# Two query tiles that share their gate and up projections in the tail of a transformer block

## The chip, the cores and the metric

The kernel runs on one core of a Trainium2 chip. The metric is the device time of one execution in microseconds; the figure given for a kernel is the median of its runs. The engines are called TensorE (PE in the profile; its weight loads are PEld), VectorE (DVE), ScalarE (ACT), GpSimd (POOL) and SyncE (SP, which issues the DMAs).

## What is computed

One transformer block with modulated layer norms, over 2048 tokens of width 512, with 32 heads of 16 and a gated MLP of width 1792, all in bf16. Cut to what matters:

```python
mod = (silu(c) @ w_mod).reshape(1, 6, 1, 512)
sa, ca, ga, sb, cb, gb = [mod[:, i] for i in range(6)]
h = layernorm(x) * (1 + ca) + sa
q, k, v = split_heads(h @ wqkv)                  # 32 heads of 16
p = softmax(q @ k.T * 16 ** -0.5)
x = x + ga * ((p @ v) @ wo)
h = layernorm(x) * (1 + cb) + sb
x = x + gb * ((gelu(h @ w_gate) * (h @ w_up)) @ w_down)
```

## The kernel before

The 2048 tokens are 16 tiles of 128. Queries are taken in six sets of 512, 512, 512, 256, 128 and 128 tokens (`SETS`, tiles 0-3, 4-7, 8-11, 12-13, 14 and 15). The heads are taken eight at a time by position in their group of four (`qd` 0 to 7). The last two sets run together over 256 columns for `qd` 0 to 5 and apart for 6 and 7. A unit of work, a set and a `qd`, is cut into score banks: one PSUM bank of 128 keys or more by 512 columns. There are six score banks (`ps_sc`), used three by three: while TensorE fills three, ScalarE takes the exponential of the other three in one ACTIVATE to the SBUF ring `E` of 24 slots. Two more banks are `ps_pv`, which gathers P times V for a unit, and `ps_mi`, which everything else shares.

Some groups of four score banks (a "quad") don't go to ScalarE: VectorE converts the scores to 16-bit integers with a scale and an offset, which read as bf16 are an approximate exponential; three further copies with shifted offsets, on VectorE or GpSimd, average the error. Which groups go this way is decided as the program is made.

The program's order is not written out by hand. A recorder keeps every instruction with its reads and writes and a rough model of when each engine would be free (`model`, `cost`). The function `stream` picks, position by position (`pos` counts score banks), what TensorE does next: the next scores, P times V of a bank that is done, a piece of side work, or a filler matmul that is thrown away (`short` asks whether the last 3.4 us had enough of them). Side work (`plan`) are generators: projections of the first half, the output projection (`side_wo`), the second layer norm and the MLP of each query set (`side_ffn`), all in the bank `ps_mi`, one after the other. A credit grows with each position and is spent with each piece of side work. VectorE's and GpSimd's pieces are `tasks`, a list of steps each; `step` takes the ready one with the lowest `urgency`.

What follows the last scores is `tail`. It has two generators, and goes on with what is left of the side work. At each turn it takes the matmul that can start first; the first generator has 300 ns of preference. With `self.whole` set, matmuls use the full array in place of four column strips. The names that matter there: `ka` is tile 14, `kb` is tile 15. `TCOL` gives their columns in the transposed norm `t2T` (256 and 384, next to each other), `prods` are their gated products, `wg`, `wu` and `wd` the resident weights of gate, up and down, loaded long before. For tile 14 the LN statistics come in the main stream; its four transposes are the side entry `side_ffn(k, EARLY)` with `EARLY = 0`, in `ps_mi`, and VectorE scales and shifts the result into `t2T`. For tile 15 `tail_end` makes the last two reciprocals (`near_end`), the output projection on top of x in score bank 4, LN, and four transposes in score bank 5 and `ps_mi`. `tail_ffn` is run for each tile by itself: chunks of four 128-column blocks of the MLP (the last of two), for each a gate bank, an up bank, ScalarE's GELU, VectorE's product, and the down matmuls of the chunk before. `down_fin` scales the sum with `gb`, adds it to x and stores the tile.

Of the kernel before, what the change touches and what calls it, by code (L numbers as in the profile page):

```python
# [5 lines left out]
ACT = mybir.ActivationFunctionType  # L6
ALU = mybir.AluOpType
BF16 = mybir.dt.bfloat16
# [5 lines left out]
P = 128  # L14
# [7 lines left out]
NFC = F // P  # L22
# [25 lines left out]
PREFER = 300  # L48
# [20 lines left out]
FLOW = NA - 2  # L69
URGENT = 6  # L70
LAG = 40
EARLY = 0
BACK = 8
END = (0, None)

# [31 lines left out]
class _Recorder:  # L107
# [181 lines left out]
    def model(self, op, t, cost):  # L289
        eng = op.eng  # L290
        if op.stream not in COMPUTE:
            self.free[eng] = t + 460
            early = t < 20000
            self.dma_free = max(t + 1400, self.dma_free) + cost / (350 if early else RATE)
            op.t1 = self.dma_free + (1500 if early else LAND)
        elif eng == "pe":
            cols, rows, tp = cost
            mode = 0 if tp is None else (1 if rows == 32 else 2)
            t = max(t, self.pe_issue)
            if self.fetched[0] % 128 == 0 and t > 20000:  # L300
                t = self.fetched[1] = max(t, self.fetched[1] + 3750)
            self.fetched[0] += 1
            if mode != self.pe_mode:
                t = max(t, self.pe_end + 105)
            q = range(16)
            if mode == 1:
                q = range(tp[0] // 8, tp[0] // 8 + 4)
            elif mode == 2:
                q = range(tp[1] // 32, 16, 4)
            t = max(t, max(self.tile_free[i] for i in q))  # L310
            end = t + max(cols, 64) / 2.4
            for i in q:
# [159 lines left out]
class _Kernel(_Recorder):  # L472
# [485 lines left out]
            self.task(steps[:1], ("rs", gi), self.after([("st2", t) for t in tiles]))  # L958
            self.task(steps[1:], ("ln2", gi), self.after([("rs", gi)] + [("ffn", gi - 1)] * (0 < gi <= FLOW) + [("ffn", FLOW)] * (gi > FLOW + 1)))

    def side_ffn(self, gi, part=None):

        q0, W = SETS[gi]
        n = W // P
        tiles = [q0 // P + i for i in range(n)]
        mi = self.mi[:, :]
        c0, t0 = BCOL[gi], TCOL[gi]
# [3 lines left out]
        kpb = 512 // W  # L971
        chunks = []
# [16 lines left out]
            load(0, i)  # L989
            load(1, i)  # L990
        yield from self.until(("ln2", gi))
        if part is not None:
            for i in range(5):
                yield from self.until(("ld", "u", i))
        for h in range(2):
            yield from self.side_t(lambda t: self.normed(gi, t), n, h,
                                   lambda dc: self.t2T[:, dc, t0:t0 + W], self.modB)
# [29 lines left out]
        def U(ci):  # L1027
# [8 lines left out]
            for b0 in range(0, m, kpb):  # L1036
# [7 lines left out]
                    self.tt("dve", prod[:, fcs[0]:fcs[0] + m, c0:c0 + W], w.rearrange("p (k n) -> p k n", k=m),  # L1044
                            g.rearrange("p (k n) -> p k n", k=m), ALU.mult)
                yield END
        nch = len(chunks) if part is None else part
        for i in range(3):
            load_down(i)
        for ci in range(nch + 1):  # L1050
# [4 lines left out]
            if ci >= 1:  # L1055
                yield from U(ci - 1)
                if ci >= nch - 1:
                    load_down(5 + ci - nch + 1)
        if part is not None:
            self.done(("part", gi))  # L1060
            return
        wd = self.wdst if flow else self.wd
        for i in range(0 if flow else 7):
            yield from self.until(("ld", "d", i))
# [12 lines left out]

    def urgency(self, tk):

        if tk[1] is None or tk[1][0] in ("den", "ld"):  # L1080
            return -1
        if tk[1][0] != "shift":
            return 1
        return 0 if self.plain[tk[1][1]] <= (URGENT if tk[1][1][3] == 512 else URG2) else 2
# [58 lines left out]
    def plan(self, ends, nsplit):  # L1143
# [19 lines left out]
        w.append((lambda: self.near_end(k, 6, self.mi[:, 0:P]), s0, s0, True))  # L1163
        w.append((lambda: self.near_end(k, 7, self.mi[:, 0:P]), s0, s0, True))
        w.append((lambda: self.side_wo(k), s0, s0, True))
        w.append((lambda: self.side_ffn(k, EARLY), s0, n - 20, True))
        res = []
        for mk, s, e, *early in w:
            self.dry = True
# [58 lines left out]
    def stream(self):  # L1228
# [133 lines left out]
        while cg <= group[units[-1]]:  # L1362
# [95 lines left out]
            if hot:  # L1458
                pv_do(hot[0])
                continue  # L1460
            if ok[0] and (ok[1] or self.pe_mode == 2 or tq is None or not mem) and not (side and self.credit > 1536 and tq is not None):
                pv_do(tp[0])
                continue
            if side:
# [131 lines left out]
    def tail(self, ka, kb):  # L1596

        self.whole = True
        self.act(self.tcol[:, 0:1], self.tcol[:, 0:1], ACT.Gelu_apprx_tanh)
        gens = [self.tail_end(kb), self.tail_ffn(ka, self.pv[:, :], range(0, 4), 0)]  # L1600
        nxt = [None] * len(gens)
        while True:
            t = self.pe_now()
# [3 lines left out]
            for i, g in enumerate(gens):  # L1607
                if g is None:
                    continue
                if nxt[i] is None:  # L1610
                    nxt[i] = next(g, 0)
                if nxt[i] == 0:
                    gens[i] = None
                elif nxt[i] is not None:
                    x = max(self.probe(nxt[i]), t + 30) - (PREFER if i == 0 and ("x1", kb) not in self.have else 0)
                    if best is None or x < best[0]:
                        best = x, i
            w = self.next_side()
# [18 lines left out]
            f, nxt[best[1]] = nxt[best[1]], None  # L1637
            f()

    def tail_end(self, k):  # L1640
        q0, W = SETS[k]
        assert W == P
        c0, tile = BCOL[k], q0 // P
# [12 lines left out]
        while self.work:  # L1656
            yield None
        for h in range(2):
            pb = (self.scp[:, 5, :], self.mi[:, :])[h]
            yield lambda h=h, pb=pb: self.transp(pb, lambda t: self.normed(k, t), 1, h)  # L1660
            for i in range(2):
                dc = 2 * h + i
                self.modulate(("act", "dve")[h], self.t2T[:, dc, TCOL[k]:TCOL[k] + W],
                              pb.bitcast(BF16)[:, W * i:W * i + W], self.modB, dc)
        yield from self.until(("x1", k))
        yield from self.tail_ffn(k, self.mi[:, :], (5, 4, 0, 1, 2, 3), 4)

    def tail_ffn(self, k, down, banks, e0):
        q0, W = SETS[k]
        c0, tile, kpb = BCOL[k], q0 // P, 512 // W  # L1670
        chunks = [range(a, min(NFC, a + kpb)) for a in range(0, NFC, kpb)]
        nb = [0]

        def up(ci, w):
            if nb[0] == 2 and k == len(SETS) - 1:
                yield from self.until(("p", k - 1, len(chunks) - 1))
            bk = self.scp[:, banks[nb[0] % len(banks)], :]
            nb[0] += 1
            for s, fc in enumerate(chunks[ci]):
                for dci in range(NDC):  # L1680
                    yield lambda s=s, fc=fc, dci=dci: self.up_mm(bk[:, W * s:W * s + W], w, fc, TCOL[k], W, dci)
            return bk
        first = 0
        if k < len(SETS) - 1:
            first = EARLY
            yield from self.until(("part", k))
        for ci in range(first):
            for fc in chunks[ci]:
                yield lambda fc=fc: self.down_mm(down, c0 // P, fc)
        for ci in range(first, len(chunks) + 1):  # L1690
            if ci < len(chunks):
                n = len(chunks[ci])
                g = self.E[:, e0 + ci, 0:W * n]
                bg = yield from up(ci, self.wg)
                self.task([("act", lambda bg=bg, g=g, n=n: self.act(g, bg[:, 0:W * n], ACT.Gelu_apprx_tanh))],
                          ("g", k, ci))
                bu = yield from up(ci, self.wu)
                yield from self.until(("g", k, ci))
                self.task([lambda bu=bu, g=g, n=n, f0=chunks[ci][0]: self.stt(
                    self.prods[c0 // P][:, f0:f0 + n, :], bu[:, 0:W * n].rearrange("p (k n) -> p k n", k=n), 2.0,  # L1700
                    g.rearrange("p (k n) -> p k n", k=n), ALU.mult, ALU.mult)], ("p", k, ci))
            if ci > first:
                yield from self.until(("p", k, ci - 1))
                if k == len(SETS) - 1:
                    self.done("down")
                for fc in chunks[ci - 1]:
                    yield lambda fc=fc: self.down_mm(down, c0 // P, fc)
        self.task([lambda: self.down_fin(down, tile)], None)


def bass_adaLN_cond__mha_block__geglu_ffn__prompt_kernel(
# [41 lines left out]
```

The softmax here doesn't subtract the row's maximum and nothing guards it: scores larger than these inputs give would overflow.

## Time and profile before

| | us |
|---|---|
| median of 5 runs (lowest to highest) | 809.32 (807.74 to 809.80) |
| the profiled execution | 809.32 |
| its span | 807.3 |
| TensorE busy | 753.0 (93%) |
| ScalarE busy | 769.7 (95%) |
| VectorE busy | 688.8 (85%) |
| GpSimd busy | 262.3 (32%) |
| last exponential ends at | 775.7 |
| last PV matmuls end at | about 777.0 |
| last matmul, by the modelled end | 803.7 |
| last store issued at | 805.1 |

The span goes from the first to the last instruction that the profile holds; 2 us lie around it. The 40 slices show three stages: a start of some 20 us with the loads at 311 GB/s, a long stretch in which ScalarE is at 9 tenths in every slice, and the last slice and a half, in which ScalarE has little to do:

```profile
PE   8999999999899998999989999999999999998988
PEld 3333333322222222222222222222333333354556
DVE  6878998987898899989898899998898897879753
ACT  4999999999999999999999999999999999999951
```

A tail of 30 us in a span of 807 is hard to see there; the stretches and the chain of waits cut by time show it.

### The profile page before, as it was taken

The page shows a single profiled execution, that of the slowest core. Times are in us where ns is not written, and L with a number is a line of the kernel's source. Part 1 is how long each engine was busy: PE and PEld are TensorE (multiplying, and loading weights), DVE is VectorE, ACT ScalarE, POOL GpSimd, SP SyncE. Part 2 cuts the span into 40 slices and gives each one's busy share as a digit, 9 for nine tenths or more (in the row PEclk, how much of TensorE's full clock was granted, in tenths as well). Part 3 has the DMA queues.
Part 4 walks back from the last instruction along what each step waited for, and adds up shares of the span by engine and source line. Part 5 has one row for each costly group of instructions (what it writes and reads, how often), then busy time and mean ns, then how long its engine had stood idle before and what let it go on. Part 6 is the DMA issues. An engine that isn't in the chain of part 4 may idle for free.

```text
span 807.3 us, 27653 instructions
## 1 busy us (share of the span) xinstructions
PE 753.0 (93%) x12359; PEld 272.8 (34%) x12359; DVE 688.8 (85%) x1252; ACT 769.7 (95%) x733; POOL 262.3 (32%) x162
## 2 busy tenths in 40 slices
PE   8999999999899998999989999999999999998988
PEld 3333333322222222222222222222333333354556
DVE  6878998987898899989898899998898897879753
ACT  4999999999999999999999999999999999999951
POOL 2100427282655351424436551333425000002100
PEclk9999999999999999999999999999999999999999
DMA  9100000000022111210022021120122221120000
GB/s 311 57 9 11 16 10 16 11 17 10 15 61 62 35 55 35 61 42 19 26 58 71 25 59 41 49 55 23 39 68 75 65 73 37 43 68 14 20 10 15
DMA packets 58617, 36.05 MB, mean 45 GB/s; under 512 B 17961, under 2 KB 55074, under 8 KB 58498
## 3 DMA queue, kind: packets, MB, share of 16 engines
q1 hardware_dynamic: 56114, 32.71, 14.8%
q8 instruction: 97, 1.59, 0.8%
q10 hardware_dynamic: 2384, 1.57, 0.7%
q14 instruction: 22, 0.18, 0.1%
HBM read 29.62 MB, written 2.61 MB: 40 GB/s over the span
## 4 chain that ended last, share of the span: by engine, by line
ACT 83%; PE 12%; DVE 3%; DMA 1%; issue 0%; SPq 0%; DVEq 0%
ACT E L379 80%; PE ps_sc L366 6%; PE ps_mi L366 3%; ACT wreg L379 3%; PE ps_pv L366 2%; DMA mreg<-in_w_mod_dram 1%; DVE mreg L391 1%; DVE wreg L383 0%; DMA rb<-scr_rec 0%; DVE dreg L391 0%; SPq L430 0%; DVE wreg L391 0%; DVE xs L383 0%; DVE hreg L391 0%; PE ps_sc L370 0%
## 5 line engine op out<-in xcount | busy, mean ns | idle before, releaser
L379 ACT ACTIVATE E<-ps_sc 128x1024 bf16<-128x1024 f32 (+2 forms) x686 | 742.4, 1267 | 15.7 <-PE ps_sc L366 13.6
L391 POOL TENSOR_SCALAR mreg<-dreg 128x2048 uint16<-128x2048 uint16 x93 | 175.1, 1897 | 270.9 <-DVE mreg L391 114.0
L391 DVE TENSOR_SCALAR dreg<-ps_sc 128x512 uint16<-128x512 f32 x258 | 174.8, 686 | 31.3 <-PE ps_sc L366 29.5
L366 PE MATMUL ps_sc<-qT,kme 32*128 32x512 bf16 (+2 forms) x1311 | 172.0, 332 | 15.1 <-ACT E L379 13.5
L366 PE MATMUL ps_sc<-qT,kmo 32*128 32x512 bf16 (+2 forms) x1316 | 173.3, 331 | 10.5 <-ACT E L379 9.7
L366 PE MATMUL ps_pv<-E,vaug 128*17 128x512 bf16 (+2 forms) x2096 | 148.9, 327 | 1.2 <-DVE vaug L400 0.8
L366 PE MATMUL ps_pv<-mreg,vaug 128*17 128x512 bf16 (+2 forms) x1768 | 124.9, 338 | 1.2 <-DVE mreg L391 0.5
L391 DVE TENSOR_SCALAR mreg<-ps_sc 128x512 uint16<-128x512 f32 x134 | 91.0, 685 | 15.3 <-PE ps_sc L366 14.8
L391 POOL TENSOR_SCALAR mreg<-mreg 128x2048 uint16<-128x2048 uint16 x38 | 71.6, 1897 | 96.1 <-DVE mreg L391 55.7
L366 PE MATMUL ps_mi<-wreg,mreg 128*32 128x512 bf16 (+1 forms) x1280 | 91.8, 372 | 2.3 <-DVE wreg L396 0.7
L366 PEld LDWEIGHTS ps_sc<-qT,kme 32*128 32x128 bf16 x1311 | 45.4, 91 | 139.4 <-ACT E L379 111.2
L366 PEld LDWEIGHTS ps_sc<-qT,kmo 32*128 32x128 bf16 x1316 | 45.8, 91 | 130.9 <-ACT E L379 110.4
L391 DVE TENSOR_SCALAR mreg<-dreg 128x2048 uint16<-128x2048 uint16 x123 | 81.1, 685 | 0.5 <-PE ps_pv L366 0.4
L366 PEld LDWEIGHTS ps_pv<-E,vaug 128*17 128x17 bf16 x2096 | 44.2, 89 | 58.1 <-issue 46.5
L366 PEld LDWEIGHTS ps_pv<-mreg,vaug 128*17 128x17 bf16 x1768 | 40.3, 89 | 35.0 <-issue 10.9
L391 DVE TENSOR_SCALAR mreg<-mreg 128x2048 uint16<-128x2048 uint16 x73 | 47.9, 684 | 4.2 <-PE ps_pv L366 4.1
L643 POOL TENSOR_SCALAR mv<-mv 128x4 f32<-128x4 f32 (+2 forms) x10 | 2.7, 269 | 128.9 <-DVE mv L423 121.5
L366 PEld LDWEIGHTS ps_mi<-wreg,mreg 128*32 128x32 bf16 x1280 | 27.3, 95 | 40.1 <-issue 16.8
L366 PE MATMUL ps_mi<-hreg,wreg 128*32 128x512 bf16 x480 | 39.9, 384 | 0.4 <-DVE vaug L400 0.2
L366 PE MATMUL ps_sc<-xs,ident 128*32 128x512 bf16 x353 | 28.9, 401 | 11.4 <-ACT E L379 11.2
L400 DVE CAST wreg<-ps_mi 128x512 bf16<-128x512 f32 x49 | 33.6, 685 | 5.8 <-PE ps_mi L366 5.6
L396 DVE SCALAR_TENSOR_TENSOR wreg<-wreg,ps_mi 128x512 bf16<-128x512 bf16 x49 | 33.4, 681 | 4.6 <-PE ps_mi L366 3.0
(151 smaller groups left out, 692.8 us busy)
## 6 DMA issues: line engine op xcount, KB each, us to landing
mreg<-in_B_w_up_dram SPq DMA_DIRECT2D x22, 256.0 KB, 3.0
mreg<-in_B_w_gate_dram SPq DMA_DIRECT2D x15, 256.0 KB, 3.0
rb<-scr_rec SPq DMA_DIRECT2D x96, 32.0 KB, 1.8
dreg<-in_B_w_down_dram SPq DMA_DIRECT2D x9, 256.0 KB, 3.3
mreg<-in_w_mod_dram SPq DMA_DIRECT2D x1, 2048.0 KB, 14.5
mreg<-in_B_w_down_dram SPq DMA_DIRECT2D x8, 256.0 KB, 2.7
out_dram<-xs SPq DMA_DIRECT2D x16, 128.0 KB, 1.7
osb<-osb SPq DMA_DIRECT2D x48, 32.0 KB, 2.0
```

Source lines behind the costliest of these rows:

```text
L366: return self.rec("pe", lambda e: e.matmul(out, lhsT, rhs, start=start, stop=stop, tile_position=tp), [lhsT, rhs], [out], cost=(n, int(rhs ...
L379: return self.rec("act", lambda e: e.activation(out, in_, func, scale=scale, **kw), rd, wr, cost=self.cost("act", out, [in_], "act"))
L391: return self.rec(eng, lambda e: e.tensor_scalar(out, a, s1, s2, **kw), rd, [out], cost=self.cost(eng, out, [a], "ts"))
L396: return self.rec("dve", lambda e: e.scalar_tensor_tensor(out, a, s, b, op0=op0, op1=op1), rd, [out], cost=self.cost("dve", out, [a, b], " ...
L400: return self.rec(eng, lambda e: e.tensor_copy(out, in_), [in_], [out], cost=self.cost(eng, out, [in_], "ts"))
L643: self.rec("pool", lambda e: e.tensor_scalar(v, v, EPS, None, op0=ALU.add), [v], [v], cost=200)
```

## The change

Tile 14's transposes leave the side work and become `tail_t`, which tile 15 uses too: tile 14 in score banks 1 and 2, tile 15 in 5 and 3. Tile 14's scaling and shifting moves to ScalarE. There is one `tail_ffn` for both tiles. It runs at most `SOLO = 2` stages of four blocks for tile 14 alone, as long as tile 15's transposes are not there; then the same stages for tile 15 alone; then the rest in stages of two blocks, with tiles 14 and 15 side by side as 256 moving columns. Down matmuls stay apart by tile, tile 14's in `ps_pv`, tile 15's in `ps_mi`, and tile 15's wait until the side work is over.

Around it: `urgency` puts tile 15's reciprocals, normalised heads and LN steps first on VectorE in the tail; the tail's first generator keeps its preference to the end; in the last `CLOSE = 48` positions of the stream, ready P times V is no longer held back for side work; and the planner's model counts a matmul of 128 columns or more on the full array as at least 160 columns and a shorter one as at least 64 (before: at least 64 for both).

The model's line reads `max(cols, 64 if mode or cols < P else 160)`, where `mode` is 0 for the full array.

```diff
-EARLY = 0
+SOLO = 2
+CLOSE = 48
...
-            end = t + max(cols, 64) / 2.4
+            end = t + max(cols, 64 if mode or cols < P else 160) / 2.4
...
     def urgency(self, tk):
 
+        if self.whole and tk[1] is not None and tk[1][0] in ("rec", "onorm", "ln2") and tk[1][1] == len(SETS) - 1:
+            return -2
...
-        w.append((lambda: self.side_ffn(k, EARLY), s0, n - 20, True))
...
-            if ok[0] and (ok[1] or self.pe_mode == 2 or tq is None or not mem) and not (side and self.credit > 1536 and tq is not None):
+            if ok[0] and (ok[1] or self.pe_mode == 2 or tq is None or not mem) and not (side and self.credit > 1536 and tq is not None and pos < nseq - CLOSE):
...
-        gens = [self.tail_end(kb), self.tail_ffn(ka, self.pv[:, :], range(0, 4), 0)]
+        gens = [self.tail_end(kb), self.tail_ffn(ka, kb)]
...
-                    x = max(self.probe(nxt[i]), t + 30) - (PREFER if i == 0 and ("x1", kb) not in self.have else 0)
+                    x = max(self.probe(nxt[i]), t + 30) - (PREFER if i == 0 else 0)
...
+    def tail_t(self, k, banks):
+
+        yield from self.until(("ln2", k))
+        for h in range(2):
+            pb = self.scp[:, banks[h], :]
+            yield lambda h=h, pb=pb: self.transp(pb, lambda t: self.normed(k, t), 1, h)
+            for i in range(2):
+                dc = 2 * h + i
+                self.modulate(("act", "dve")[h * (k == len(SETS) - 1)], self.t2T[:, dc, TCOL[k]:TCOL[k] + P],
+                              pb.bitcast(BF16)[:, P * i:P * i + P], self.modB, dc)
+        self.done(("t2", k))
...
-        while self.work:
-            yield None
-        for h in range(2):
-            pb = (self.scp[:, 5, :], self.mi[:, :])[h]
...
-        yield from self.until(("x1", k))
-        yield from self.tail_ffn(k, self.mi[:, :], (5, 4, 0, 1, 2, 3), 4)
+        yield from self.tail_t(k, (5, 3))
+
+    def tail_ffn(self, ka, kb):
+
+        yield from self.tail_t(ka, (1, 2))
+        for i in range(5):
+            yield from self.until(("ld", "u", i))
+        nb = [0, 0]
+        count = {ka: 0, kb: 0}
+        downs = {ka: self.pv[:, :], kb: self.mi[:, :]}
+
+        def up(w, fcs, ks):
+            c, W = TCOL[ks[0]], P * len(ks)
+            banks = (0, 1, 2, 5, 3, 4) if ("x1", kb) in self.have else (0, 1, 2)
+            bk = self.scp[:, banks[nb[0] % len(banks)], :]
+            nb[0] += 1
+            for s, fc in enumerate(fcs):
+                for dci in range(NDC):
+                    yield lambda s=s, fc=fc, dci=dci: self.up_mm(bk[:, W * s:W * s + W], w, fc, c, W, dci)
+            return bk
+
+        def split(x, fcs, ks, i):
+            return x[:, 0:P * len(fcs) * len(ks)].rearrange("p (k t n) -> p k t n", t=len(ks), n=P)[:, :, i, :]
+
+        def down(fcs, ks, e):
+            yield from self.until(("p", e))
+            for k in ks:
+                while k == kb and self.work:
+                    yield None
+                if k == kb:
+                    self.done("down")
+                for fc in fcs:
+                    i = count[k]
+                    count[k] += 1
+                    yield lambda k=k, fc=fc, i=i: self.mm(downs[k], self.prods[BCOL[k] // P][:, fc, :],
+                                                          self.wd[fc // 2][:, fc % 2, :], start=i == 0, stop=i == NFC - 1)
+                if count[k] == NFC:
+                    self.task([lambda k=k: self.down_fin(downs[k], SETS[k][0] // P)], None)
+
+        def stage(fcs, ks, last):
+            e, n = nb[1], len(fcs) * len(ks) * P
+            nb[1] += 1
+            g = self.E[:, e, :]
+            bg = yield from up(self.wg, fcs, ks)
+            self.task([("act", lambda: self.act(g[:, 0:n], bg[:, 0:n], ACT.Gelu_apprx_tanh))], ("g", e))
+            bu = yield from up(self.wu, fcs, ks)
+            yield from self.until(("g", e))
+            self.task([lambda i=i, k=k: self.stt(self.prods[BCOL[k] // P][:, fcs[0]:fcs[-1] + 1, :], split(bu, fcs, ks, i), 2.0,
+                                                 split(g, fcs, ks, i), ALU.mult, ALU.mult) for i, k in enumerate(ks)], ("p", e))
+            if last:
+                yield from down(*last)
+            return fcs, ks, e
+        last, alone = None, []
+        for a in range(0, 4 * SOLO, 4):
+            if ("t2", kb) in self.have:
+                break
+            alone.append(range(a, a + 4))
+            last = yield from stage(alone[-1], (ka,), last)
+        yield from self.until(("t2", kb))
+        yield from self.until(("x1", kb))
+        for fcs in alone:
+            last = yield from stage(fcs, (kb,), last)
+        for a in range(4 * len(alone), NFC, 2):
+            last = yield from stage(range(a, a + 2), (ka, kb), last)
+        yield from down(*last)
```

More of the change, by code (lines that the diff above doesn't have):

```diff
@@ L959, in side_wo, with side_ffn @@
             self.task(steps[1:], ("ln2", gi), self.after([("rs", gi)] + [("ffn", gi - 1)] * (0 < gi <= FLOW) + [("ffn", FLOW)] * (gi > FLOW + 1)))
-    def side_ffn(self, gi, part=None):
+    def side_ffn(self, gi):
         q0, W = SETS[gi]
@@ L991, in side_ffn @@
         yield from self.until(("ln2", gi))
-        if part is not None:
-            for i in range(5):
-                yield from self.until(("ld", "u", i))
         for h in range(2):
@@ L1046, in U @@
                 yield END
-        nch = len(chunks) if part is None else part
+        nch = len(chunks)
         for i in range(3):
@@ L1058, in side_ffn @@
                     load_down(5 + ci - nch + 1)
-        if part is not None:
-            self.done(("part", gi))
-            return
         wd = self.wdst if flow else self.wd
@@ L1642, in tail_end @@
         assert W == P
-        c0, tile = BCOL[k], q0 // P
+        tile = q0 // P
         bank = self.scp[:, 4, :]
@@ L1655, in tail_end @@
         self.task([("act", lambda: self.act(self.xs[:, tile, :], bank, ACT.Copy))], ("x1", k))
-        while self.work:
-            yield None
-        for h in range(2):
-            pb = (self.scp[:, 5, :], self.mi[:, :])[h]
[L1660 to L1664, printed above, removed]
@@ L1665, in tail_end @@
-        yield from self.until(("x1", k))
-        yield from self.tail_ffn(k, self.mi[:, :], (5, 4, 0, 1, 2, 3), 4)
[L1668 to L1676, printed above, removed]
+        yield from self.tail_t(k, (5, 3))
@@ L1677, in up @@
+    def tail_ffn(self, ka, kb):
[8 more added lines that the diff above has]
+            banks = (0, 1, 2, 5, 3, 4) if ("x1", kb) in self.have else (0, 1, 2)
             bk = self.scp[:, banks[nb[0] % len(banks)], :]
             nb[0] += 1
-            for s, fc in enumerate(chunks[ci]):
+            for s, fc in enumerate(fcs):
@@ L1680, in up @@
                 for dci in range(NDC):
-                    yield lambda s=s, fc=fc, dci=dci: self.up_mm(bk[:, W * s:W * s + W], w, fc, TCOL[k], W, dci)
+                    yield lambda s=s, fc=fc, dci=dci: self.up_mm(bk[:, W * s:W * s + W], w, fc, c, W, dci)
             return bk
[L1683 to L1704, printed above, removed]
-                    self.done("down")
-                for fc in chunks[ci - 1]:
-                    yield lambda fc=fc: self.down_mm(down, c0 // P, fc)
@@ L1708, in tail_ffn @@
-        self.task([lambda: self.down_fin(down, tile)], None)
+        def split(x, fcs, ks, i):
[6 more added lines that the diff above has]
+                if k == kb:
+                    self.done("down")
+                for fc in fcs:
[5 more added lines that the diff above has]
+                    self.task([lambda k=k: self.down_fin(downs[k], SETS[k][0] // P)], None)
```

## The prediction

> **What bounds the kernel now.** I read the page's chain of waits first, then ScalarE's busy time over the long middle stretch, then the last 30 us in three views: busy time with granted clock by stretch, the chain in order of time, and TensorE's timeline.
>
> ```profile
> ACT 83%; PE 12%; DVE 3%; DMA 1%; issue 0%; SPq 0%; DVEq 0%
> ...
> 25.00:775.72 750.72, 706.65 (x11697) 244.41 (x11698) 657.42 (x1174) 748.35 (x700) 254.26 (x144) 1.00 0.14 38
> 777.00:780.20 3.20, 3.18 (x27) 1.51 (x15) 2.81 (x6) 0.23 (x2) 0.00 (x0) 1.00 0.03 5
> 780.20:783.20 3.00, 0.85 (x7) 0.43 (x7) 2.55 (x9) 0.00 (x0) 0.80 (x2) 1.00 0.13 44
> 783.20:786.60 3.40, 3.38 (x32) 3.16 (x32) 1.34 (x4) 1.89 (x4) 0.00 (x0) 0.51 0.00 0
> 786.60:803.70 17.10, 17.09 (x225) 13.53 (x222) 5.92 (x10) 3.75 (x7) 0.00 (x0) 1.00 0.01 2
> 752.50:764.30 11.80, 10.31 (x290) 5.28 (x293) 8.44 (x17) 11.67 (x12) 3.79 (x2) 1.00 0.07 15
> ```
>
> The columns of the stretches are start:end, length, then busy time of TensorE, its weight loads, VectorE, ScalarE and GpSimd, the granted clock, DMA share and GB/s. From 25 us to 775.72 us ScalarE is busy for 748.35 of 750.72 us: the exponentials set the time, and only 2.4 us of it are gaps. ScalarE's last exponential ends there. After it TensorE sets the end, and it has two losses. Between 780.2 and 783.2 us it works for 0.85 of 3.00 us: a **hole** of 2.15 us. In the next 3.4 us it is busy all the time, but at a granted clock of 0.51: 3.38 x 0.49 = 1.66 us lost. From 786.6 to 803.7 us it is full, at full clock.
>
> The chain in order of time (start, length, what) says who holds the hole open:
>
> ```profile
> 779.10 0.66 PE ps_mi L366 x3
> 779.77 0.02 issue
> 779.79 0.70 DVE wreg L383
> 780.49 0.02 issue
> 780.51 0.42 DVE xs L383
> 780.94 0.62 DVE st L419
> ...
> 781.76 0.49 DVE wreg L391 x2
> 782.26 0.05 issue
> 782.30 0.30 PE ps_mi L370 x2
> ...
> 791.36 1.79 PE ps_sc L366 x32
> 793.15 0.86 PE ps_pv L366 x4
> ```
>
> Tile 13's last down matmuls in the bank `mi` end, its two closing VectorE operations follow, and only then can tile 14 (`ka`) have its transposes in `mi`, each pair waiting for VectorE to scale and shift the one before. Yet tile 14's norm was written by 775.05 us (the 0.41 us operation on VectorE that starts at 774.64). So tile 14's projections, ready in principle, begin only at 782.43, beside tile 15's own LN chain, whose transposes start at 784.00. The last two lines give prices: 32 full-array matmuls of 128 columns take 1.79 us, **56 ns** each; four of 512 take 0.86, **215 ns** each.
>
> **The change, part by part.** The profiled execution took 809.32 us, span 807.3, and 809.32 is also the median shown, so I subtract from 809.32 directly.
>
> Removed: the side entry that made tile 14's transposes in `mi`. The four transposes, and four VectorE operations of 0.28 to 0.35 us, leave VectorE between 781.68 and 783.22; the same four transposes come back in the tail, into score banks 1 and 2, with four ScalarE operations. The last exponential has left those banks at 775.72 and the table load is over at 777.02, so the transposes can follow the last PV matmuls at 777.0 (0.3 us, the row at 782.30). ScalarE's row for this work, two in 0.80 us from 784.53, mean 456 ns, steps by 0.34: four take 3 x 0.34 + 0.46 = 1.5 us, so tile 14 is ready at about 777.5 + 1.5 = 779.0. ScalarE is idle from 777.24 to 784.04, so this costs nothing; without that cover it would be 1.5 us.
>
> Fill: tile 14 goes alone through up to two stages of four chunks, 64 matmuls x 56 ns = 3.58 us, and one stage's four down matmuls, 0.86: 4.44 us of work that exists from 779.0 on. The other work of TensorE up to the hole (two reciprocal sums, 0.68; identity and output projection, 0.86 + 0.43; tile 13's down matmuls, 1.08; the transposes, 0.3) is 3.35 us from 777.07. Together they reach 777.07 + 3.35 + 4.44 = 784.9, past tile 15's transposes at 784.0. So the hole can close: **-2.15**. With no stretch of low activity I also expect the clock to hold: **-1.66**. The row for that is 752.5 to 764.3, where TensorE is busy 10.31 of 11.80 us, with waits of 0.48 to 0.74 us, at clock 1.00.
>
> The Trainium skill, "TensorE: Matmul & The Clock Gate", section "Why this matters for your kernels", speaks against that second gain: it puts the fall to half rate down to idle gaps of over about 3 us, and the longest single gap here is 1.48 us. Taken by the letter the half clock has another cause, and the time would be 1.66 us above my sum. The trace has 1.23 busy us in the 3.4 before the fall, so I go by low activity in a window.
>
> Sharing: the last six chunks of both tiles run as three stages of 16 matmuls over 256 columns, 48 in place of 96. No full-array row of 256 columns is shown; bounds are 56 and 215 ns. The nearest row is the column-split form (`ps_mi<-wreg,mreg 128*32 128x256`, x32 from 748.58 to the next start at 749.46): eight full equivalents in 0.88 us, 110 ns. 48 x 0.110 = 5.28 against 96 x 0.056 = 5.38: **-0.1**, at most -2.7 and at worst +4.9 by the bounds; I take the nearest row, since two of 128 cost the same 112.
>
> The same page, section "Back-to-back issue gap", gives about 81 ns for a 128-column matmul in a stream with weight loads, and 262 cycles for 256 columns. As an estimate from it, sharing would save 2.5 us and not 0.1. The row says 56 ns with weight loads in between, so the page's price isn't met here.
>
> Given back: (a) Now both tiles end together. The last down matmuls of `ka` end 0.43 us before `kb`'s, and `ka`'s closing pair on VectorE (0.70 + 0.03 + 0.42, rows at 802.65 and 803.38) stands ahead of `kb`'s. Before, the last VectorE end was 805.05, 1.36 after TensorE's modelled end at 803.69; now -0.43 + 1.15 + 0.1 + 1.15 = 1.97 after it: **+0.6**. (b) The last stage's two products (0.42 us rows of 128x256, 0.36 apart, with 0.07 and 0.1 around them: 0.95) must be done before its downs, and the previous stage's four downs cover 0.86: **+0.1**. (c) Tile 15's scaled transposes come 1.3 us after its transposes start (784.00 to 785.33), that is between 784.4 and 785.3; the fill ends between 784.4 and 784.9. A stall of 0 to 0.9: **+0.4**, the middle. If fillers cover it the clock is safe, but not the time.
>
> The urgency edit lets tile 15's reciprocals, norms and LN steps go first on VectorE. Tile 13's closing pair (780.86 could be 780.25) and tile 14's scalings (0.3) stood in the chain; a product of 0.69 us can now stand there instead. Bounds -0.9 to +0.7; taken as 0, because TensorE has work for that time anyway. What queues behind the new wait of the joint stages (`t2` and `x1` of tile 15) is tile 15's and the shared work on TensorE alone.
>
> Letting PV go ahead of side work in the last 48 positions only reorders. Best: fewer than the 64 PV matmuls (0.89 us) remain after the last exponential, at most -0.5. Worst: the nine down matmuls of tile 13 that now run before 777 slip behind, 9 x 0.215 = +1.9. I take 0, nearest to a swap of equal work. A transpose priced at 160 columns in the planner is no instruction; it shifts planned times and can reshuffle the long stretch. There, gaps could yield at most 2.4 us, or a group of four score banks could move between ScalarE and VectorE. By the page's exp rows (412.7/420 for two banks, 372.3/257 for three: 0.48 a bank) a group is worth **1.9 us**. Sign unknown; I take 0.
>
> DMAs, GpSimd operations and SP's queue keep their number: nothing is moved past them but the two output stores, both now at the end and already overlapping (1.59 us for both).
>
> Sum: -2.15 - 1.66 - 0.1 + 0.6 + 0.1 + 0.4 = **-2.8**: 806.5 us, span 804.5.
>
> **Rivals.**
> (1) *The exponentials grow*. The reshuffled plan hands fewer score banks to VectorE, which is 85% busy with no rule that keeps the number. Each lost group costs 1.9 us of an engine that has 2.4 us of gaps in 750. One gives 808.4; from two (810.3) the change is slower than before; three give 812.2. Against it: a 14 ns shift per transpose is small beside any 1.1 us exponential.
> (2) *The hole stays in part*: tile 14's gates come late, or tile 15's chain gets products in front of it. With 1.1 us of hole and the half clock left: -1.05 - 0.1 + 0.7 = -0.4, so 808.9. For it: TensorE's order is fixed in advance by modelled times. Against: 4.4 us of work for 3 us.
> (3) *The exponentials shrink* by one group: 804.6.
> (4) *The change doesn't do what it says*: if tile 15's transposes are ready early, no solo stage runs. But its LN chain needs 6.9 us after 777.1, so I fold this into (2).
>
> **How the numbers follow.** Forecast 0.50 (own range 805.0 to 808.2); rival 1 0.22; rival 2 0.13; rival 3 0.15. About 0.2% (1.6 us) is what a measurement can tell from no change: 807.7 to 810.9 is "same". The forecast gives 0.43 faster and 0.07 same; rival 1 0.02, 0.06 and 0.14 slower; rival 2 0.02, 0.10, 0.01; rival 3 0.15 faster. Sums: 0.62, 0.23, 0.15. The range, 803.4 to 810.6, leaves out the part of rival 1 from three groups on, and two gained groups at the other end.
>
> **What would show it.** Right: TensorE's busy share from 780 to 784 over 0.9, the granted clock 1.00 up to the end, first gate matmuls of tile 14 near 779, 256-column matmuls 110 ns apart, TensorE's end some 23 us after the last PV, two closing pairs back to back on VectorE. Wrong: the last exponential ends elsewhere than 775.7 by over 1 us, or a half-clock stretch remains in the tail. Then the count of score banks on VectorE (436 now: 258, 134, 30 and 14 in its four `uint16<-128x512 f32` rows) tells rival 1 or 3.

## The result and the profile after

The changed kernel takes 812.68 us (median), the kernel before 808.76 in the same comparison: ratio 1.0045, 95% interval 1.0036 to 1.0054. By the ratio it is slower by 3.6 us. The forecast was 806.5, the range 803.4 to 810.6.

The first view is the chain's shares and two stretches of the changed kernel, cut at its last exponential (columns as above). The second has the same cut for the kernel before.

```profile
ACT 89%; PE 8%; DMA 1%; DVE 1%; issue 0%; SPq 0%; DVEq 0%
...
25.00:786.17 761.17, 710.53 (x11715) 243.12 (x11715) 643.87 (x1150) 757.16 (x698) 238.05 (x135) 1.00 0.14 37
786.17:813.10 26.93, 21.63 (x237) 16.31 (x237) 11.92 (x24) 8.35 (x16) 0.80 (x2) 1.00 0.03 11
```

```profile
25.00:775.74 750.74, 706.67 (x11697) 244.43 (x11698) 657.44 (x1174) 748.35 (x700) 254.26 (x144) 1.00 0.14 38
775.74:807.30 31.56, 25.76 (x351) 19.60 (x341) 14.04 (x29) 7.13 (x13) 0.80 (x2) 0.94 0.04 14
```

ScalarE's share of the chain rises from 83% to 89%. Its last exponential ends 10.4 us later (786.17 against 775.74), and it works 8.8 us more before that (757.16 against 748.35). What follows is 4.6 us shorter (26.93 against 31.56), at a full clock. So the tail got shorter and the long stretch before it longer, though of that stretch the change edits only a price in the planner and, near its end, the order of P times V. This profiled execution took 815.29 us, 2.6 over its kernel's median; some of the 10.4 is that execution's own (ScalarE's gaps are 4.0 us here, 2.4 before). Executions of one kernel spread with their mean granted clock: those of the changed kernel go from 811.46 us at 0.999 to 815.29 at 0.994.

Where ScalarE's extra work comes from is read in VectorE's groups, which convert score banks in its place. The changed kernel first, then the kernel before:

```profile
L392 DVE TENSOR_SCALAR dreg<-ps_sc 128x512 uint16<-128x512 f32 x244 | 165.0, 685 | 33.2 <-PE ps_sc L367 31.3
L392 DVE TENSOR_SCALAR mreg<-ps_sc 128x512 uint16<-128x512 f32 x124 | 84.7, 686 | 16.3 <-PE ps_sc L367 14.9 <-POOL mreg L392 0.2
L392 DVE TENSOR_SCALAR dreg<-ps_mi 128x512 uint16<-128x512 f32 x32 | 21.9, 685 | 8.3 <-PE ps_mi L367 8.1
L392 DVE TENSOR_SCALAR mreg<-ps_mi 128x512 uint16<-128x512 f32 x16 | 11.0, 684 | 2.1 <-PE ps_mi L367 2.0
```

```profile
L391 DVE TENSOR_SCALAR dreg<-ps_sc 128x512 uint16<-128x512 f32 x258 | 174.8, 686 | 31.3 <-PE ps_sc L366 29.5
L391 DVE TENSOR_SCALAR mreg<-ps_sc 128x512 uint16<-128x512 f32 x134 | 91.0, 685 | 15.3 <-PE ps_sc L366 14.8
L391 DVE TENSOR_SCALAR dreg<-ps_mi 128x512 uint16<-128x512 f32 x30 | 20.5, 685 | 5.4 <-PE ps_mi L366 5.1
L391 DVE TENSOR_SCALAR mreg<-ps_mi 128x512 uint16<-128x512 f32 x14 | 9.6, 685 | 2.3 <-PE ps_mi L366 2.3
```

244 + 124 + 32 + 16 = 416 banks, 104 groups of four; before it was 436, 109 groups. The five groups went to ScalarE: 8.8 us over five is 1.8 each in this execution.

TensorE's timeline of the changed tail (start, length, operation, count, idle before it):

```profile
788.07 0.23 PE L367 MATMUL ps_sc<-wreg,qT 128*128 128x128 bf16 x1 [0.55 <-ACT wreg L380]
...
792.91 0.40 PE L371 MATMUL ps_sc<-ident,E 128*128 128x128 bf16 x4 [0.50 <-DVE E L392]
...
800.03 1.04 PE L367 MATMUL ps_sc<-wreg,qT 128*128 128x256 bf16 x8
800.90 1.04 PE L367 MATMUL ps_sc<-wreg,hreg 128*128 128x256 bf16 x8
```

The long hole is gone: behind the last P times V two waits of 0.55 and 0.50 us are left. Eight matmuls of 256 columns start 0.87 us apart as a block, 109 ns each.

### The profile page after: what moved, and what is told of

Same layout as the page of the kernel before. It is cut to its first block, busy times and chain, and to the rows that moved or that the text cites. A ratio compares the mean times of both kernels' runs of the same rounds, so it can differ in the third digit from the quotient of the medians.

```text
span 813.1 us, 27449 instructions
## 1 busy us (share of the span) xinstructions
PE 752.6 (93%) x12270; PEld 268.2 (33%) x12270; DVE 672.9 (83%) x1224; ACT 779.6 (96%) x734; POOL 246.1 (30%) x153
## 4 chain that ended last, share of the span: by engine, by line
ACT 89%; PE 8%; DMA 1%; DVE 1%; issue 0%; SPq 0%; DVEq 0%
ACT E L380 86%; PE ps_sc L367 5%; ACT wreg L380 3%; PE ps_mi L367 2%; PE ps_pv L367 1%; DMA mreg<-in_w_mod_dram 1%; DMA den<-scr_den 0%; PE ps_sc L371 0%; DVE wreg L384 0%; DVE kmo L401 0%; ACT L380 0%; SPq L431 0%; DVE xs L384 0%; DVE E L392 0%; DVE vaug L401 0%
## 5 line engine op out<-in xcount | busy, mean ns | idle before, releaser
L380 ACT ACTIVATE E<-ps_sc 128x1024 bf16<-128x1024 f32 (+2 forms) x683 | 751.4, 1295 | 18.1 <-PE ps_sc L367 16.4
L392 POOL TENSOR_SCALAR mreg<-dreg 128x2048 uint16<-128x2048 uint16 x88 | 165.7, 1897 | 269.5 <-DVE mreg L392 89.2
L392 DVE TENSOR_SCALAR dreg<-ps_sc 128x512 uint16<-128x512 f32 x244 | 165.0, 685 | 33.2 <-PE ps_sc L367 31.3
L367 PE MATMUL ps_pv<-mreg,vaug 128*17 128x512 bf16 (+2 forms) x1680 | 120.4, 338 | 2.1 <-DVE mreg L392 0.7
L392 POOL TENSOR_SCALAR mreg<-mreg 128x2048 uint16<-128x2048 uint16 x34 | 64.2, 1898 | 190.1 <-DVE mreg L392 63.3
L392 DVE TENSOR_SCALAR mreg<-ps_sc 128x512 uint16<-128x512 f32 x124 | 84.7, 686 | 16.3 <-PE ps_sc L367 14.9
L392 DVE TENSOR_SCALAR mreg<-dreg 128x2048 uint16<-128x2048 uint16 x119 | 78.8, 687 | 1.7 <-PE ps_pv L367 1.5
L367 PEld LDWEIGHTS ps_pv<-mreg,vaug 128*17 128x17 bf16 x1680 | 37.8, 89 | 35.2 <-issue 12.9
L367 PE MATMUL ps_sc<-xs,ident 128*32 128x512 bf16 (+1 forms) x373 | 31.7, 402 | 16.3 <-ACT E L380 15.9
L384 DVE TENSOR_TENSOR wreg<-wreg 128x1024 bf16<-128x1024 bf16 (+1 forms) x56 | 34.1, 615 | 0.3
```

Of the source, the lines that this page charges most:

```text
L367: return self.rec("pe", lambda e: e.matmul(out, lhsT, rhs, start=start, stop=stop, tile_position=tp), [lhsT, rhs], [out], cost=(n, int(rhs ...
L380: return self.rec("act", lambda e: e.activation(out, in_, func, scale=scale, **kw), rd, wr, cost=self.cost("act", out, [in_], "act"))
L384: return self.rec(eng, lambda e: e.tensor_tensor(out, a, b, op), [a, b], [out], cost=self.cost(eng, out, [a, b], "tt"))
L392: return self.rec(eng, lambda e: e.tensor_scalar(out, a, s1, s2, **kw), rd, [out], cost=self.cost(eng, out, [a], "ts"))
```

## The experiments

Every run goes with its own runs of the kernel before. "Groups" are counted in its profile as above; "last exp." is the end of the last exponential and "tail" the time from there to the end of the span, in the profiled execution. The last exponential of one stream ends up to 2 us apart in different executions (774.68 to 776.64 in e3, e6 and e7, which have one stream), and a profiled execution can lie up to 2.6 us from its kernel's median (815.29 for after, 812.62 for e8, 803.07 for e10). The ratio is the firmest column; a tail is that of one execution.

| kernel | price | CLOSE | tail code | groups | last exp. | tail | median | ratio to before (95%) |
|---|---|---|---|---|---|---|---|---|
| before | 64 | no | old | 109 | 775.74 | 31.56 | | |
| after | 160 | 48 | new | 104 | 786.17 | 26.93 | 812.68 | 1.0045 (1.0036-1.0054) |
| e1 | 64 | 48 | new | 110 | 773.04 | 31.06 | 805.96 | 0.9971 (0.9959-0.9983) |
| e2 | 160 | no | old | 104 | 784.28 | 26.12 | 812.71 | 1.0058 (1.0045-1.0071) |
| e3 | 64 | no | new | 109 | 774.68 | 29.02 | 805.57 | 0.9979 (0.9964-0.9994) |
| e4 | 165 | 48 | new | 110 | 772.52 | 34.28 | 809.77 | 1.0023 (1.0009-1.0037) |
| e5 | 64 | 48 | old | 110 | 774.66 | 33.64 | 810.95 | 1.0014 (0.9996-1.0033) |
| e6 | 64 | no | new, no solo stage | 109 | 776.08 | 34.52 | 812.61 | 1.0026 (1.0004-1.0047) |
| e7 | 64 | no | new, not shared | 109 | 776.64 | 29.16 | 807.21 | 0.9962 (0.9944-0.9981) |
| e8 | 64, other draw | no | old | 106 | 784.61 | 25.89 | 810.12 | 1.0007 (0.9984-1.0030) |
| e9 | 160 | no | new | 104 | 782.86 | 26.94 | 812.33 | 1.0043 (1.0028-1.0059) |
| e10 | 64 | 96 | new | 108 | 774.36 | 26.64 | 805.46 | 0.9957 (0.9938-0.9975) |
| e11 | 160, other draw | no | new | 107 | 781.01 | 26.99 | 809.54 | 1.0006 (0.9996-1.0016) |
| e12 | 64 | 96 | new, not shared | 108 | 777.93 | 26.77 | 804.86 | 0.9949 (0.9934-0.9964) |

### Which edit lengthened the stream

e1 undoes one line of the change; e2 makes that one line alone in the kernel before:

```diff
-            end = t + max(cols, 64 if mode or cols < P else 160) / 2.4
+            end = t + max(cols, 64) / 2.4
```

> The change with one line undone: the planner prices full-array matmuls at 64 columns or more as before; the whole tail and CLOSE stay. Theory A (the new price reshuffled the plan, VectorE got 104 groups of four score banks and not 109, at 1.9 us each, and the tail itself gains): about 110 groups, last exponential near 774 us, and with the tail's gain of 3 to 4.6 us a time of 803 to 805. Theory B (CLOSE, that is PV ahead of side work at the end, or the tail's missing side entry lengthened the stream; the price is harmless): last exponential still near 786 and a time near 812.7.

> The kernel before with nothing but the new price of 160 columns in the planner. Theory A: 104 groups, last exponential near 785.5, old tail of 31.6 us behind it: 817 to 818, slower than the whole change. Theory B: no change, 808 to 809.5. Theory C (the price makes the plan's times truer and so helps the stream): below 808.

e1 ran 805.96, 2.3 us under before, with 110 groups and the last exponential at 773.04. e2 ran 812.71, 4.7 us over, with 104 groups. The price line by itself is the loss: theory B and theory C fall. But e2 was expected at 817 to 818 with the old tail of 31.6 us, and its tail is 26.12 us:

```profile
25.00:784.28 759.28, 707.94 (x11706) 242.88 (x11702) 645.05 (x1155) 757.04 (x699) 238.18 (x136) 1.00 0.14 37
784.28:810.40 26.12, 21.44 (x276) 16.71 (x281) 12.24 (x24) 7.13 (x13) 0.80 (x2) 0.98 0.03 11
```

That is the old tail code, 5.4 us shorter than in the kernel before, with 21.44 us of TensorE work in place of 25.76. While ScalarE makes five more groups' exponentials, TensorE waits for score banks and gets the side work done that was left over before; tile 13's bank is free, tile 14's transposes go into it at 782.8, and the hole doesn't form. The last exponential ends 8.5 us later and the tail is 5.4 shorter in these two executions; by the ratio 4.7 us of the 8.5 stay. So the longer stream gets about half of its price back in the tail.

### The tail by itself

e3 is the change with the old price and without CLOSE, so its stream is that of before.

```diff
-            end = t + max(cols, 64 if mode or cols < P else 160) / 2.4
+            end = t + max(cols, 64) / 2.4
...
- ... and not (side and self.credit > 1536 and tq is not None and pos < nseq - CLOSE):
+ ... and not (side and self.credit > 1536 and tq is not None):
```

> The change with the old price and without CLOSE, so that the stream up to the last exponential is that of before (109 groups, 775.7 us) and the tail alone differs. The prediction's sum for the tail: -2.8, so 806. The trace of after suggests more (26.9 us from the last exponential to the end in place of 31.6): 804.2. A tail that gains only because the longer stream had finished tile 13's side work: -2 or less, 807.

It ran 805.57, ratio 0.9979: -1.7 us by the ratio, -0.5 to -2.9 by its interval. Its tail in three stretches:

```profile
778.00:782.00 4.00, 3.93 (x62) 3.43 (x60) 2.98 (x7) 1.34 (x3) 0.80 (x2) 1.00 0.00 0
782.00:788.80 6.80, 6.60 (x83) 5.17 (x85) 2.61 (x6) 2.49 (x5) 0.00 (x0) 1.00 0.01 2
788.80:789.70 0.90, 0.14 (x1) 0.00 (x0) 0.69 (x2) 0.00 (x0) 0.00 (x0) 1.00 0.00 0
```

TensorE is full where the hole was, at clock 1.00. The third line is a stall that the prediction had not: 0.79 us in front of tile 15's first down matmuls. They share the bank `mi` with tile 13's, whose last three were left until 788.13, and wait for tile 13's closing VectorE operation.

e6 takes the solo stages from e3 (`SOLO = 0`), e7 takes the sharing from it.

```diff
-SOLO = 2
+SOLO = 0
```

> The new tail on the old stream (old price, no CLOSE) with SOLO = 0: tile 14 runs nothing alone, every stage waits for tile 15 and is shared. If the gain of the tail-only run (805.6) comes from filling the hole: TensorE empty between about 779 and 783.5 in the tail, some 3.6 us of it, 808.5 to 810, half clock or not by whether fillers step in. If it comes from sharing the 256 columns: 805.5 or less.

```diff
         for a in range(4 * len(alone), NFC, 2):
-            last = yield from stage(range(a, a + 2), (ka, kb), last)
+            for k in (ka, kb):
+                last = yield from stage(range(a, a + 2), (k,), last)
```

> The new tail on the old stream with no sharing: after the two stages of each tile alone, the rest runs in stages of two blocks for tile 14 and then tile 15, 128 columns each. By the rows (56 ns against 109 ns for 256 columns): 805.6 plus 0.1, within noise; tile 14 ends a stage earlier, which may take off up to 0.6. If weight loads set the pace of 128-column matmuls (81 ns each): plus 2.5, 808.

e6 loses 0.47% against e3 (1.0026 against 0.9979), and its trace shows the hole and what follows it:

```profile
780.60:784.70 4.10, 0.17 (x1) 0.00 (x0) 2.72 (x5) 0.00 (x0) 0.80 (x2) 0.83 0.09 32
783.10:789.90 6.80, 4.74 (x23) 3.16 (x24) 1.77 (x5) 1.89 (x4) 0.58 (x1) 0.51 0.02 7
789.90:793.00 3.10, 3.05 (x25) 2.34 (x24) 1.15 (x4) 0.60 (x1) 0.00 (x0) 0.97 0.00 0
```

A wait of 3.96 us, up to 784.73; still inside it, from 783.2 on, the clock is at half, for 6.8 us. So without the solo stages that fill this time the new tail gains nothing. The urgency and preference edits were not run by themselves. e7's interval (0.9944 to 0.9981) overlaps e3's, and so do e12's and e10's, a second pair with and without sharing: sharing 256 columns, the edit that the change is named for, has no effect that these runs can tell. The Trainium skill ("TensorE: Matmul & The Clock Gate", "Back-to-back issue gap") gives 81 ns for a 128-column matmul in a stream with weight loads; as an estimate from it, e7 would have been 2.5 us slower than e3. In e7's trace eight of them take 0.45 us (795.64 to 796.09), 56 ns each.

### The price or the draw

If the new price only reshuffles the plan (each plan that comes out is called a draw here), another price or another unrelated number should give another count. e4 sets 165 for 160. e8 is the kernel before with a DMA's landing time in the planner at 1320 ns for 1300; e11 is e9 with the same number at 1280.

```diff
-            end = t + max(cols, 64 if mode or cols < P else 160) / 2.4
+            end = t + max(cols, 64 if mode or cols < P else 165) / 2.4
```

> The whole change with the price at 165 columns in place of 160. Theory A says the price matters only as a draw of the plan: about 110 groups and 803 to 806. Theory D (dearer transposes by themselves make the plan worse, step by step): 812 to 814, like 160 or a little worse.

```diff
-LAND = 1300
+LAND = 1320
```

> The kernel before with one unrelated number of the planner changed, a DMA's landing time of 1320 ns for 1300: another draw of the same stream at the old price, with 106 groups for 109. Group theory at 1.9 us a group: 808.1 + 5.7 = 813.8. At the 0.9 us a group that the price-only run shows (4.6 us for five): 810.9. If the dearer transposes were the cause and not the groups: 808.

```diff
-LAND = 1300
+LAND = 1280
```

> The new price of 160 and the new tail, without CLOSE, in another draw of the plan: the landing time of a DMA in the planner at 1280 ns for 1300. As planned 107 groups for 104 and no side work left at the end. If the price itself is harmless and only the draw costs: last exponential near 778, and 26.9 us behind it: 805 to 807. If dearer transposes cost by themselves: near the 812.3 of the same kernel in the first draw.

The counts are 110, 106 and 107: a dearer transpose doesn't by itself cost groups, and the old price can lose three. So 104 was one draw of a plan in which small edits shift later choices: 160 and 165 columns are 2 ns apart in the model. But the times did not follow the groups. e4 has the earliest last exponential of all (772.52) and still takes 809.77, where 803 to 806 was expected. Its tail says why (TensorE's timeline):

```profile
786.59 1.46 PE L367 MATMUL ps_mi<-dreg,hreg 128*128 128x512 bf16 x6
788.84 1.90 PE L367 MATMUL ps_mi<-xs,hreg 128*128 128x512 bf16 x8 [0.79 <-DVE wreg L384]
790.57 1.46 PE L367 MATMUL ps_mi<-dreg,hreg 128*128 128x512 bf16 x6
792.82 1.04 PE L367 MATMUL ps_mi<-xs,hreg 128*128 128x512 bf16 x4 [0.79 <-DVE wreg L384]
```

The first three lines are down matmuls of tiles 12 and 13: 24 of their 28 come after 785.7 us, the first four just ahead of these lines. Tile 15's own begin in the last line. Twice the bank waits 0.79 us for VectorE's closing operation on the tile before. In e8 three groups fewer cost nothing that can be told (-0.16% to +0.30%), and the tail is 25.89 us instead of 31.56. e11 came out between its two expectations: 809.54, ratio 1.0006. Against e9 (1.0043), the same kernel in another draw, three more groups are worth 0.37%, 3.0 us. Its last exponential was not at 778 but at 781, with 4.8 us of gaps on ScalarE (751.25 busy of 756.01) where the kernel before has 2.4.

One rival stays open. With the new tail, every plan made at the new price (ratios 1.0045, 1.0043, 1.0006, and 1.0023 at 165) is slower than every one at the old price (0.9949 to 0.9979, e6 without solo stages aside), and e8 lost three groups at the old price without a loss that can be told, as was expected if the dearer transposes and not the groups were the cause. A fixed cost of the price can't be all of it, since e9 and e11 differ by 0.37% at one price; whether a dearer transpose makes plans worse on the average, these few draws can't say.

### CLOSE, and whether the gains add

e5 adds only CLOSE to the kernel before; e9 takes only CLOSE from the changed kernel.

```diff
- ... and not (side and self.credit > 1536 and tq is not None):
+ ... and not (side and self.credit > 1536 and tq is not None and pos < nseq - 48):
```

> The kernel before with nothing but PV ahead of side work in the last 48 positions. Group theory (each group of score banks that VectorE takes is worth 1.9 us to the end): 110 groups for 109, so 806.2. Backlog theory (TensorE has a fixed amount of work, and what the stream doesn't do before the last exponential it does after it): last exponential some 1.6 us earlier, but all 14 down matmuls of tile 13 behind it, 3 us in place of 1.1, so 808 to 809, no gain.

> The whole change without CLOSE: the new price with the new tail alone, the cell that is missing beside before, price only (812.7), tail only (805.6) and the whole change. If gains and losses add: 812.7 - 2.5 = 810.2. If the longer stream had already closed the hole (the price-only trace has TensorE nearly full after the last exponential, at clock 1.00), the new tail has nothing to win there: 812 to 813.3.

e5: 110 groups, no gain (1.0014, interval 0.9996 to 1.0033). The backlog theory holds: all fourteen down matmuls of tile 13 come after the last exponential, and the tail is 33.64 us, with 27.28 us of TensorE work. e9: 812.33, ratio 1.0043. Beside e2 (1.0058) the new tail brings 0.15% on the long stream, beside before it brings 0.21% on the short one; these times can't tell whether gains and losses add. The traces say more:

```profile
784.61:810.50 25.89, 21.78 (x292) 17.07 (x297) 12.49 (x26) 7.13 (x13) 0.80 (x2) 1.00 0.04 12
```

```profile
782.86:809.80 26.94, 21.79 (x234) 16.45 (x238) 11.92 (x24) 8.36 (x16) 0.80 (x2) 0.97 0.03 11
```

```profile
774.36:801.00 26.64, 21.79 (x234) 16.46 (x238) 12.06 (x25) 8.36 (x16) 0.80 (x2) 1.00 0.05 16
```

These are the tails of e8 (old code), e9 and e10 (new code). Wherever no side work is left, the old tail takes 25.9 and 26.1 us (e8, e2) and the new one 26.6 to 27.0 (after, e9, e10, e11): no gain there, 0.5 to 1.1 us more, from one execution each. Apart from e6 with its hole, what makes a tail long is what the stream left over: TensorE is busy for 25.6 to 27.7 us in the tails of before, e1, e4 and e5, which last 31.1 to 34.3 us, and for 21.4 to 22.3 in those that last 25.9 to 27.0.

### A version that beats both

e10 is the change with the old price and CLOSE over 96 positions, so that PV is cleared earlier and the side work is over in time; e12 also drops the sharing, as in e7.

```diff
-            end = t + max(cols, 64 if mode or cols < P else 160) / 2.4
+            end = t + max(cols, 64) / 2.4
...
-CLOSE = 48
+CLOSE = 96
```

> The change at the old price with CLOSE = 96 in place of 48. As planned it has 108 groups and no side work left when the tail begins. Backlog theory: that is what counts, not the number of groups; no stall on the bank of tile 13's down matmuls and a shorter tail, 804 to 805.5, a little under the tail-only run. Group theory: one group fewer than tail only, 807.5.

> The old price with CLOSE = 96, the new tail and no sharing: each tile's stages of two blocks apart. Sharing is worth 0.1 us by the rows and costs 0.6 at the end, where two tiles close together: 804.5 to 805.5, equal to or a little under the shared form (805.5). If sharing helps TensorE: 807.

e10 has 108 groups, one under before, and takes 805.46 (0.9957); e12 takes 804.86 (0.9949). Both beat before and after; between them, and from e1, e7, the intervals overlap.

## Why the prediction was wrong

- **The failed step** is the one on the planner's price: "A transpose priced at 160 columns in the planner is no instruction; it shifts planned times and can reshuffle the long stretch. [...] Sign unknown; I take 0." That line alone costs 0.58%, 4.7 us (e2) and five groups that went from VectorE to ScalarE. Its mechanism was written down as rival 1, with 0.22, and "a 14 ns shift per transpose is small beside any 1.1 us exponential" spoke against it. The count fell by five groups, where one to three had been priced. Rival 1's figure for three, 812.2, lies beside the measured 812.68 by luck: five groups at its own price give 806.5 + 9.5 = 816.0. A choice made by comparing modelled times can turn on less than 14 ns (2 ns lie between the changed kernel and e4, 104 and 110 groups).
- **The price of a group** was 1.9 us. ScalarE's busy time from 25 us to its last exponential is 748.35, 753.32, 757.04 and 745.44 us with 109, 106, 104 and 110 groups (before, e8, e2, e4): 1.7 us for each of e2's five and e8's three, 2.9 for e4's one. So the term was right to about a tenth for ScalarE. (Its rows count some time twice: the forms of two and three banks add up to 785.0 us, the line of all forms has 742.4; by that a bank takes 0.46 us, not 0.48.) It was wrong for the end: e2's 4.7 us over five groups is 0.9 each, e8's three cost nothing that can be told. The sum treated the stream and the tail as separate. They are not: TensorE has a store of work, and each us by which ScalarE ends later lets it finish some of that first, until none is left.
- **The hole and the half clock** were read rightly, and the fill works as written (e3 against e6; in e3 the first gate matmuls of tile 14 start 3.2 us behind the last exponential, 3.3 by the forecast). The tail's term was -2.8; e3 gives -1.7 with -0.5 to -2.9, so it holds, at the edge. It missed the 0.79 us at the bank `mi`. The stall taken as +0.4 shows ahead of tile 15's transposes and not behind them: 0.16 us in e3, 0.50 in the changed kernel. In the changed kernel there was no hole left to fill, because its stream was longer: e2 and e8 close it with the old code.
- **Low activity or single gaps.** The rule of the Trainium skill ("TensorE: Matmul & The Clock Gate", "Why this matters for your kernels"), about 3 us idle, was weighed against a reading by window. In e5 the old tail's longest wait is 1.40 us, and the clock is at 0.50 again behind it (784.3 to 785.0); e3, with no such stretch, stays at 1.00 from its last exponential until TensorE is done. That fits the reading by window, and e6 does too: one long wait behind dense work, and the clock falls 2.4 us into it, with 0.96 us busy in the 3.4 before. In the long stretch it falls behind still shorter waits: in the kernel before at 342.9 us (1.84 of 3.4 us busy, longest wait 0.95), in the changed one at 121.1 (2.27, 0.52) and 612.6 (2.06, 0.95). So no gap of 3 us is needed in these traces. But the busy share doesn't decide it alone: at the same place of the same stream e3 and e6, with 1.84 and 1.85 us busy, stay at 1.00, and e3 falls at 269.4 behind 1.96 us where the kernel before, with 1.96 too, doesn't. What decides between executions stays open.
- **Sharing at -0.1** and 110 ns for 256 columns: 109 ns in the trace, and no effect in e7 and e12.
- **Two closing pairs at the end, +0.6**: VectorE ends 2.01 us after TensorE's modelled end (810.89 against 808.88), where the forecast had 1.97. In the chain of the changed kernel the last down matmuls give way at 808.47 to four VectorE operations one behind the other:

```profile
808.49 0.70 DVE wreg L384
809.20 0.02 issue
809.22 0.43 DVE xs L384
...
809.75 0.70 DVE wreg L384
810.45 0.02 issue
810.47 0.42 DVE xs L384
```

- **CLOSE taken as 0**, bounds -0.5 to +1.9: nothing that can be told by itself (e5), and the mechanism of the upper bound, tile 13's down matmuls behind the last exponential, is what happened there.

## What to carry to other kernels

When a program's order is made by a planner, a number in its model is an edit of the whole kernel: before any tail is read, count what each engine was given, and compare edits over several draws, not one. When one engine feeds a stretch and another has work stored up behind it, the gain of ending the first earlier stops where the store begins; sum the second engine's work from one end to the other rather than adding stretches. A hole in a tail is worth filling only in the version that still has it.

## What the runs showed that was not expected

One execution's ScalarE gaps up to the last exponential differ by more than the program explains: 2.4 us before, 4.0 in the changed kernel, 4.8 in e11, 6.3 in e8 (753.32 busy of 759.61). In e8 the granted clock averaged 0.98 from 500 to 784.6 us, and ScalarE waited for TensorE up to 1.44 us at a time. The dips belong to the execution and not to the program alone: the mean clock of e8's twelve runs goes from 0.991 to 1.000, and its fastest run, 806.84 us, is the one at 1.000. Why one execution has them and another has not was not settled.

The half clock in e6 lasts 6.8 us, twice the 3.4 us behind the shorter waits of the kernel before. In its first half (783.2 to 786.6) TensorE is busy for only 1.44 of 3.40 us, the rest of the wait and the start of the shared stages; in the second it is full, as the kernel before is in its single half, and then the clock returns in both.
